# One bf16 place per token instead of two halves of a rank in a routed two-layer kernel

## Chip, core and metric

The kernel runs on one core of a Trainium2 chip. The metric is device time in microseconds, the median of several runs.

## What is computed

Agent attention over 4 sequences of 11456 tokens with 128 channels and 49 agents gives `attn`. Every token whose score against `w_skip` is positive then goes through one of 8 experts, the one with the largest gate logit; the others keep their row.

```python
a2k = sm(agents, k); agent_v = a2k @ v
q2a = sm(q, agents)
attn = q2a @ agent_v
do_compute = attn @ w_skip > 0
xc = attn[do_compute]
e_idx = argmax(xc @ w_gate)
gate_w = softmax(xc @ w_gate)[e_idx]
h = maximum(xc[mask] @ w1[e], 0)
y[mask] = gate_w[mask] * (h @ w2[e])
out[do_compute] = xc + y
```

## The kernel before

A batch is 128 partitions times 90 columns of tokens (`NC` = 90); a token's place in memory is partition x 90 + column. The kernel has two stages.

In the **attention stage** (`attention`) a hand-written order (`ORDER`) walks over chunks of six columns. In one step PE makes the scores of one chunk of keys and one of queries, sums values, and mixes queries (`query_mix`, L446) into the one tile `ps_x`, which DVE divides out and so frees (`query_norm`, L454 and L462). The words `rt` in that order take one step each of the routing generators in `queue`: `codes` finds each token's expert, `count` runs a cumulated sum over the mask of the experts (L540) and gets from it, per partition, the tokens of each expert up to a column (`oin`) and their number (`n`), and `routing` (L566) makes what the expert stage looks up. For this, PE sums `n` over the partitions below and over all (L582). From the sums come the number of 128-token units of each expert (`cnt`), the blocks' starts (`bi`), and for each partition and expert the rank at which it begins (`first`). Adding the starts to the cumulated sums and masking gives every token's rank within its batch (`rk`); POOL does this for the first 72 columns (L604 to L611), DVE for the last 18 (L628, L629). A rank needs two bf16 numbers (`twob`, L635 and L636). The product with `diff` (L646) takes the difference from partition to partition, and DVE stores it in `drow` (L657).

While the last batch is routed, PE works through `items`, a fixed list of products of two blocks of 384 tokens of expert 7 (`layer1`, L739, and `layer2`, L746) that were looked up early (`early`). `static(n)` says how far into that list PE goes before the next routing product stands in its queue: 18 items before the counts (L582), 26 before the `diff` product. A barrier ends the stage, behind ACT's last copy (L751).

The **expert stage** (`experts`) takes blocks of 384 tokens, three units of 128. SP copies for each block the table `drow` of its batch, the starts `first` and the wanted ranks `rank` into `db`, `rf` and `rr` (`fetch`, L988). DVE copies `db` to `dbs` and compares rank and start (`match`, L1085), which gives for each token a column of ones for the partitions that begin at or before it (`hit`). PE multiplies `hit` with the table (`ident_mm`, L1271): the differences add up to the row of ranks of the partition that holds the token, and one column counts up to that partition's number. There are two products per unit, one for each half:

```python
t.matmul(id_ps[:, h, :n], lhsT=m, rhs=dbs[:, h, :n], start=True, stop=False)
w = t.matmul(id_ps[:, h, :n], lhsT=m, rhs=dbs[:, h, n:], start=False, stop=True)
```

DVE compares the row with the wanted rank to find the column (`select_column`, L1096), and makes the token's index from partition and column (`select_token`, L1102 and L1104; `select_id`, L1109). A rank that is not there gets an index out of bounds. POOL gathers the rows by these indices two blocks ahead (L1213) and scatters results (L1227). Around the lookup, PE makes the two layers of the block, three products for each because values are split in two parts (L1296, L1302), ACT takes the upper part `hh` (L1187) and DVE the lower part `hl` (L1122).

DVE's order in a block (`body`, L1150) is: `hl` twice, the selections, `hl`, the token, `hl`, the index, the result of the block before, `hl` four times, the split of x (L1118), `match` for the next block. PE's (`block`, L1307) is: four parts of layer 1, the turned result, the lookup products, then layers 2 and 1 in turn, the transposition of the next x, the rest of layer 2.

Of the kernel before, what the change touches and what calls it, by code (L numbers as in the profile page):

```python
# [8 lines left out]
F32 = mybir.dt.float32  # L9
F32R = mybir.dt.float32r  # L10
BF16 = mybir.dt.bfloat16
# [6 lines left out]
P = 128  # L18
# [12 lines left out]
ROUND = 1.5 * 2.0**23 * P  # L31
# [32 lines left out]
class Shapes:  # L64
# [3 lines left out]
    def __init__(self, b, n):  # L68
# [7 lines left out]
        self.KU = self.NC + NE  # L76
# [15 lines left out]
class Persist:  # L92


    def __init__(self, nc, sh):
# [15 lines left out]
        self.db = over("db", [P, NB, 2 * (sh.NC + 1)], BF16)  # L111
# [10 lines left out]
        self.drow = a("drow", [P, sh.B, 2 * (sh.NC + 1)], BF16).ap()  # L122
        self.first = a("first", [P, sh.B * NE + 1, NB], F32).ap()
# [7 lines left out]
        self.rf, self.rr = (a(x, [P, 2 * NB], F32).ap() for x in ("rf", "rr"))  # L131
# [11 lines left out]
def attention(nc, tc, sh, io, ps):  # L143
# [10 lines left out]
    with ExitStack() as ctx:  # L154
# [55 lines left out]
        while at < sh.NC:  # L210
            n = next((n for n in range(1, sh.NC - at) if sh.COLS[at + n] != sh.COLS[at] + n), sh.NC - at)
            iota(ps.jot[:, at : at + n], [[1, n]], 1 + sh.COLS[at], 0)
# [3 lines left out]
        nc.vector.memset(ps.first, float(INVALID))  # L216
# [4 lines left out]
        nc.vector.memset(ps.drow, 0.0)  # L221
        nc.vector.memset(ps.drow[:, :, sh.NC], 1.0)
        for b in range(1, sh.B):
            x = ps.drow[:, b, 2 * sh.NC + 1 :]
            nc.vector.tensor_scalar(x, ps.ident[:, 0:1], float(P * b), None, op0=ALU.mult)
# [340 lines left out]
        def routing(b):  # L566
# [7 lines left out]
            if not last:  # L574
# [16 lines left out]
            starts = ps.first[:, b * NE : (b + 1) * NE, :]  # L591
            start = starts[:, :, 0]
            v.scalar_tensor_tensor(out=starts, in0=bi[:, :NE].unsqueeze(2).to_broadcast([P, NE, NB]), scalar=float(P),
                                   in1=pt[:, :NE].unsqueeze(2).to_broadcast([P, NE, NB]), op0=ALU.mult, op1=ALU.add)
            yield
            a = [rt.tile([P, NE], F32, name=f"a{i}") for i in range(2)]
            v.tensor_tensor(out=a[0], in0=start, in1=oin0[:, :NE], op=ALU.subtract)
            v.tensor_tensor(out=a[1], in0=start, in1=n0, op=ALU.add)
# [793 lines left out]
```

## Time and profile before

| | us |
|---|---|
| median of 3 runs (lowest, highest) | 720.91 (720.17, 721.12) |
| the profiled execution | 720.13 |
| its span, first to last instruction | 718.4 |
| busy: PE | 683.7 |
| busy: DVE | 500.4 |
| busy: ACT | 369.4 |
| busy: POOL | 361.0 |

The span is what the trace covers; 1.7 us of the execution lie around it. A matmul's end is modelled, so the starts of successive products tell more than their durations. PE's weight loads are listed as an engine of their own (PEld) and overlap the products. An idle time in brackets stands before the instruction of its row, with what ended it. The attention stage ends at 356 us; the expert stage has 37 blocks from 358 us on.

### The profile page before, as it was taken

What the parts mean: (1) busy time and instruction counts of PE and PEld (TensorE: products, weight loads), DVE (VectorE), ACT (ScalarE), POOL (GpSimd) and SP (SyncE); (2) the same over time, 40 slices, a digit from 0 to 9 for tenths busy, and PEclk for the clock granted to TensorE, in tenths of its full rate; (3) what the DMA queues carried; (4) which work ended last, traced back from release to release, by engine and by line L of the source; (5) the groups of instructions that cost most, each with busy time, mean ns of one, the idle gap of its engine ahead of it and who ended that gap; (6) DMA issues with size and microseconds to landing.
All of it is one profiled execution on the core that took longest, in us unless ns stands there. A gap on an engine that the chain in (4) does not pass through costs nothing. (4 is left out here: it accounts for less than half of the span.)

```text
span 718.4 us, 18098 instructions
## 1 busy us (share of the span) xinstructions
PE 683.7 (95%) x5447; PEld 635.5 (88%) x5447; DVE 500.4 (70%) x1694; ACT 369.4 (51%) x1036; POOL 361.0 (50%) x457
## 2 busy tenths in 40 slices
PE   6999999999989899889799999999999999999995
PEld 6988989898878788776489999999999999999995
DVE  4423445666679789887567777787777777777784
ACT  2443555545444555665245555555555555555552
POOL 3455323232424443442176666666666666666663
PEclk9999999999999999999999999999999999999998
DMA  8999989999988968672122222122222222221210
GB/s 314 388 388 396 328 290 363 332 321 299 372 277 288 314 212 274 242 261 104 52 58 63 54 50 56 53 56 56 60 56 60 60 60 56 56 60 51 53 40 18
DMA packets 80350, 123.83 MB, mean 172 GB/s; under 512 B 35798, under 2 KB 43994, under 8 KB 80288
## 3 DMA queue, kind: packets, MB, share of 16 engines
q1 hardware_dynamic: 63872, 84.76, 36.4%
q10 hardware_dynamic: 8928, 23.79, 8.5%
q0 software_dynamic: 7488, 14.54, 6.7%
q8 instruction: 29, 0.48, 0.3%
q14 instruction: 33, 0.27, 0.1%
HBM read 87.18 MB, written 31.50 MB: 165 GB/s over the span
## 5 line engine op out<-in xcount | busy, mean ns | idle before, releaser
L1187 ACT ACTIVATE hh<-h 128x384 fp32r<-128x384 f32 x296 | 145.0, 491 | 97.2 <-ACTq L936 92.8
L1122 DVE SCALAR_TENSOR_TENSOR hl<-h,hh 128x384 fp32r<-128x384 f32 x296 | 155.6, 551 | 45.1 <-DVEq L936 42.1
L1213 POOL DMA_INDIRECT xg<-out_dram,ids x108 | 110.8, 1026 | 83.9 <-issue 73.2
L1227 POOL DMA_INDIRECT out_dram<-xo,sid x117 | 116.4, 995 | 45.3 <-issue 34.5
L1302 PE MATMUL y<-hh,w 128*128 128x384 f32 x512 | 137.1, 349 | 0.0
L425 ACT ACTIVATE qe<-ps_s,qm 128x49 f32<-128x49 f32 x360 | 75.7, 311 | 116.8 <-DVE qm L419 116.8
L1296 PE MATMUL h<-xh,w 128*128 128x384 f32 x512 | 130.8, 337 | 1.1 <-PEq L936 1.1
L333 PE MATMUL ps_s<-agT,ld 128*128 128x128 f32 x960 | 124.5, 284 | 5.7 <-DMA ld<-in_k_dram 5.7
L333 PEld LDWEIGHTS ps_s<-agT,ld 128*128 128x128 f32 x960 | 114.2, 195 | 12.9 <-issue 7.1
L1296 PEld LDWEIGHTS h<-xh,w 128*128 128x128 f32 x512 | 92.5, 188 | 1.6 <-issue 1.6
L1302 PEld LDWEIGHTS y<-hh,w 128*128 128x128 f32 x512 | 89.0, 189 | 0.1
L1296 PE MATMUL h<-xl,w 128*128 128x384 f32 x256 | 86.3, 337 | 0.0
L1302 PE MATMUL y<-hl,w 128*128 128x384 f32 x256 | 86.0, 336 | 0.0
L349 DVE TENSOR_TENSOR run<-scores,run 128x294 f32<-128x294 f32 x56 | 28.7, 512 | 81.3 <-ACT scores L344 77.9
L446 PE MATMUL ps_x<-av,eT 50*128 50x138 f32 x720 | 58.8, 294 | 10.5 <-DVE G L462 9.3
L446 PEld LDWEIGHTS ps_x<-av,eT 50*128 50x128 f32 x720 | 47.0, 186 | 21.9 <-issue 12.4
L462 DVE TENSOR_TENSOR xs<-ps_x,qr 128x768 f32<-128x768 f32 x60 | 57.5, 959 | 9.1 <-DMA out_dram<-xs 5.1
L333 PE MATMUL ps_s<-agT,lds 128*128 128x128 f32 x480 | 60.7, 279 | 0.0
L333 PEld LDWEIGHTS ps_s<-agT,lds 128*128 128x128 f32 x480 | 56.0, 192 | 2.9 <-issue 0.7
L505 POOL COPY xs<-gs 128x6 f32<-128x6 f32 x60 | 10.5, 205 | 75.2 <-issue 49.1
L1296 PEld LDWEIGHTS h<-xl,w 128*128 128x128 f32 x256 | 48.1, 188 | 0.0
L1183 ACT ACTIVATE yT<-y 128x384 f32<-128x384 f32 x37 | 18.2, 492 | 58.1 <-ACTq L936 58.1
(202 smaller groups left out, 1105.7 us busy)
## 6 DMA issues: line engine op xcount, KB each, us to landing
out_dram<-xs ACTq DMA_DIRECT2D x60, 387.0 KB, 5.3
ld<-in_q_dram SPq DMA_DIRECT2D x44, 384.0 KB, 5.0
ld<-in_v_dram SPq DMA_DIRECT2D x38, 387.0 KB, 5.3
ld<-in_k_dram SPq DMA_DIRECT2D x36, 384.0 KB, 6.0
lds<-in_k_dram SPq DMA_DIRECT2D x24, 384.0 KB, 6.6
lds<-in_v_dram SPq DMA_DIRECT2D x22, 387.0 KB, 5.4
ld<-in_moe_w_dram SPq DMA_DIRECT2D x24, 256.0 KB, 5.4
lds<-in_q_dram SPq DMA_DIRECT2D x16, 384.0 KB, 5.2
```

Of the source, the lines that this page charges most:

```text
L333: r.append(ten.matmul(pt[:, t * NA : t * NA + P], lhsT=xT[:, t * P : (t + 1) * P], rhs=agT[:, b, :], start=True, stop=True))
L349: vec.tensor_tensor(out=run, in0=stored(n), in1=run, op=ALU.max)
L425: act.activation(qes[n % PAR["qe"]][:, t, :NA], s[:, t, :], AF.Exp, bias=mx[:, t : t + 1])
L446: ten.matmul(px[:, h, t, :], lhsT=eT[s, t * P : (t + 1) * P], rhs=st["av", b][s, :], start=True, stop=True)
L462: vec.tensor_tensor(out=out[:r, h, j, :], in0=px[:r, h, j, w], op=ALU.mult, in1=rs[:r, h, j].unsqueeze(3).to_broadcast(list(px[:r, h, j, w ...
L1122: v.scalar_tensor_tensor(out=hl[:, f], in0=h_ps[f % HB], scalar=0.0, in1=hh[:, f], op0=ALU.max, op1=ALU.subtract).then_inc(sem["HL"], 1)
L1183: s.activation(yT, y_ps, AF.Copy).then_inc(sem["YS"], 1)
L1187: s.activation(hh[:, f], h_ps[f % HB], AF.Relu).then_inc(sem["HH"], 1)
L1213: g.indirect_dma_start(out=xg[n % TURN][:, h, :], out_offset=None, in_=out, in_offset=bass.IndirectOffsetOnAxis(ap=ids[:, n % TURN, h : h ...
L1227: g.indirect_dma_start(out=out, out_offset=bass.IndirectOffsetOnAxis(ap=sid[:, n % 2, h : h + 1], axis=0), in_=xo[:, n % 2, h, :], in_offs ...
L1296: w = t.matmul(h_ps[f % HB], lhsT=ps.w1[e][wx][:, cs], rhs=x, start=(n == 0), stop=(n == 2))
L1302: w = t.matmul(y_ps, lhsT=ps.w2[e][wx][:, f, :], rhs=h[:, f], start=(f == 0 and n == 0), stop=(f == FC - 1 and n == 2))
```

## The change

A token is no longer looked up by its rank among all tokens of its batch, but by its place among the tokens of its partition, counted over experts. That is at most 90, so one bf16 number holds it. For each batch, expert and partition a record of three numbers (`rec`) takes the place of `first`: how many tokens of this expert the partitions below have, how many all have, and a shift, the step from partition to partition in what must be taken off the wanted rank to get the place. The shift comes out of the same `diff` product, which has 8 columns more for it (98 instead of 180 in all). The blocks' starts, the ranks' starts and the split into halves go; POOL's two sums no longer need the counts of all partitions and move ahead of them; two additions (`rhs`, `every`) and a copy (`rec`) come in, and `routing` takes fewer steps of the order for a batch.

```diff
+            rhs = rt.tile([P, NC + NE], BF16, name="rhs")
+            every = rt.tile([P, NE], F32, name="every")
+            v.tensor_tensor(out=rhs[:, NC:], in0=oin0[:, 1:], in1=oin1[:, 1:], op=ALU.add)
+            v.tensor_tensor(out=every, in0=n0, in1=n1, op=ALU.add)
+            big = part[0][0]
+            ahead = oin1[:, :NE].unsqueeze(2).to_broadcast([P, NE, NA_])
...
+                static(20)
+            else:
+                pool.tensor_tensor(out=big, in0=big, in1=ahead, op=ALU.add)
+                pool.tensor_tensor(out=big, in0=big, in1=mask[0], op=ALU.mult)
                 yield
                 yield
-            if last:
-                static(18)
             pt = ps_e.tile([P, 512], F32, name="ps_e")
...
-            bi = rt.tile([P, NE + 1], F32, name="bi")
-            v.memset(bi[:, 0:1], 0.0)
-            v.tensor_tensor_scan(bi[:, 1:], onesb[:, :NE], cnt, 0.0, ALU.mult, ALU.add)
...
-            v.tensor_tensor(out=a[0], in0=start, in1=oin0[:, :NE], op=ALU.subtract)
-            v.tensor_tensor(out=a[1], in0=start, in1=n0, op=ALU.add)
-            v.tensor_tensor(out=a[1], in0=a[1], in1=oin1[:, :NE], op=ALU.subtract)
...
+            rec = ps.rec[:, b * NE : (b + 1) * NE, :]
+            v.tensor_copy(rec[:, :, :2].rearrange("p e x -> p x e"), pt[:, : 2 * NE].rearrange("p (x e) -> p x e", x=2))
...
-            v.tensor_scalar(twob[:, 0, :], rk, ROUND, -ROUND, op0=ALU.add, op1=ALU.add)
-            v.tensor_tensor(out=twob[:, 1, :], in0=rk, in1=twob[:, 0, :], op=ALU.subtract)
...
-                static(26)
+                static(27)
...
-            ten.matmul(pd[:, : 2 * NC], lhsT=diff, rhs=twob.rearrange("p x j -> p (x j)"), start=True, stop=True)
+            ten.matmul(pd[:, : NC + NE], lhsT=diff, rhs=rhs, start=True, stop=True)
...
-            v.tensor_copy(dr, pd[:, : 2 * NC].rearrange("p (x j) -> p x j", x=2))
+            v.tensor_copy(ps.drow[:, b, :NC], pd[:, :NC])
+            v.scalar_tensor_tensor(out=rec[:, :, 2], in0=pd[:, NC : NC + NE], scalar=-1.0, in1=every, op0=ALU.mult, op1=ALU.add)
...
-                v.tensor_copy(dbs, db).then_inc(sem["RF"], NB)
+                v.tensor_copy(dbs[:, :, : sh.NC + 1], db).then_inc(sem["RF"], NB)
+                at = slice((n - 1) % 2 * NB, (n - 1) % 2 * NB + NB)
+                v.tensor_tensor(out=past, in0=rr[:, at], in1=rf[:, at, 1], op=ALU.is_gt).then_inc(sem["V1"], 1)
+                v.tensor_copy(dbs[:, :, sh.NC + 1], rf[:, at, 2])
                 for h in range(NB):
-                    x = record(n, h)
-                    w = v.tensor_scalar(hit[:, h * P : (h + 1) * P], ps.iota, rr[:, x], rf[:, x], op0=ALU.add, op1=ALU.is_ge)
+                    if h == NB - 1:
+                        take(v, "V1")
+                        v.scalar_tensor_tensor(out=want, in0=past, scalar=float(INVALID), in1=rr[:, at], op0=ALU.mult, op1=ALU.add)
+                    x = at.start + h
+                    w = v.tensor_scalar(hit[:, h * P : (h + 1) * P], ps.iota, rr[:, x : x + 1], rf[:, x, 0:1], op0=ALU.add, op1=ALU.is_ge)
...
+            def select_rank():
                 take(v, "IDP")
+                v.tensor_tensor(out=goal, in0=want, in1=id_ps[:, :, sh.NC + 1], op=ALU.subtract).then_inc(sem["V1"], 1)
...
-                    t.matmul(id_ps[:, h, :n], lhsT=m, rhs=dbs[:, h, :n], start=True, stop=False)
-                    w = t.matmul(id_ps[:, h, :n], lhsT=m, rhs=dbs[:, h, n:], start=False, stop=True)
+                    w = t.matmul(id_ps[:, h, : sh.NC + 2], lhsT=hit[:, h * P : (h + 1) * P], rhs=dbs[:, h, :],
+                                 start=True, stop=True)
```

In `fetch`, SP's copy of the table has 91 numbers a partition and unit instead of 182, that of the record three instead of one. The early lookups (`early`) change in the same way: of their two products a unit, the second has one column instead of 91.

PE's queue at the end of the attention stage, before: `ps_a`, `ps_s` and `ps_x` are written by the list of fixed products (`layer2`, `layer1`), `ps_e` by the routing.

```order
L582 MATMUL ps_e<-n_4356,onesb 128x8
L746 MATMUL ps_a<-ld_93,ld_88 128x384
L739 MATMUL ps_s<-run,ld_92 128x384
L746 MATMUL ps_a<-ld_95,ld_88 128x384
L739 MATMUL ps_s<-run,ld_92 128x384
L746 MATMUL ps_a<-ld_95,ld_88 128x384
L739 MATMUL ps_s<-run,ld_92 128x384
L746 MATMUL ps_x<-ld_89,ld_94 128x384
L646 LDWEIGHTS diff
L643 TENSOR_LOAD cnt
L644 TENSOR_LOAD cnt
L646 MATMUL ps_e<-twob,diff 128x180
```

And with the change:

```order
L593 MATMUL ps_e<-n_4336,onesb 128x8
L732 MATMUL ps_a<-ld_95,ld_88 128x384
L725 MATMUL ps_s<-run,ld_92 128x384
L732 MATMUL ps_a<-ld_95,ld_88 128x384
L725 MATMUL ps_s<-run,ld_92 128x384
L732 MATMUL ps_x<-ld_89,ld_94 128x384 x2
L630 LDWEIGHTS diff
L627 TENSOR_LOAD cnt
L628 TENSOR_LOAD cnt
L630 MATMUL ps_e<-rhs,diff 128x98
```

Between the counts and the `diff` product stand six products of the list instead of seven, and ahead of the counts two more than before (20 items instead of 18).

DVE's queue in one block of the expert stage, before (`junk` is the column selection, `t` the token, `xo` the result of the block before):

```order
L1122 SCALAR_TENSOR_TENSOR hl<-h,hh 128x384 x2
L1096 SCALAR_TENSOR_TENSOR junk,jp<-id,rr,jot 128x90 x3
L1122 SCALAR_TENSOR_TENSOR hl<-h,hh 128x384
L1102 SCALAR_TENSOR_TENSOR t<-id,jp 128x3
L1104 TENSOR_SCALAR t<-jp 128x3
L1122 SCALAR_TENSOR_TENSOR hl<-h,hh 128x384
L1109 SCALAR_TENSOR_TENSOR ids<-t 128x3
...
L1118 TENSOR_TENSOR xl<-x,xh 128x384
L1087 COPY dbs<-db 128x546
L1090 TENSOR_SCALAR hit<-iota,rr,rf 128x128 x3
```

And with the change:

```order
L1109 SCALAR_TENSOR_TENSOR hl<-h,hh 128x384 x2
L1085 TENSOR_TENSOR goal<-want,id 128x3
L1109 SCALAR_TENSOR_TENSOR hl<-h,hh 128x384
L1090 SCALAR_TENSOR_TENSOR junk,jp<-id,goal,jot 128x90 x3
L1109 SCALAR_TENSOR_TENSOR hl<-h,hh 128x384
L1096 SCALAR_TENSOR_TENSOR ids<-id,jp 128x3
...
L1071 COPY dbs<-db 128x3x91
L1073 TENSOR_TENSOR past<-rr,rf 128x3
L1074 CAST dbs<-rf 128x3
L1080 TENSOR_SCALAR hit<-iota,rr,rf 128x128 x2
L1078 SCALAR_TENSOR_TENSOR want<-past,rr 128x3
L1080 TENSOR_SCALAR hit<-iota,rr,rf 128x128
```

`goal` stands where the selections were, the selections where the token's two operations were, and three operations on three numbers stand between the table's copy and the last `hit`.

POOL's queue in the third batch around the two sums of the routing (`cum`), before; `shared` and `late` are the low parts of the weights of experts 6 and 7:

```order
L492 TENSOR_TENSOR G<-G,top 128x12x8
L320 TENSOR_TENSOR late<-ld_90,late 128x512
L505 COPY xs<-gs 128x6 x2
L610 TENSOR_TENSOR cum_3649<-cum_3649,a_3909 128x576
L611 TENSOR_TENSOR cum_3649<-cum_3649,mask_191 128x576
L320 TENSOR_TENSOR late<-ld_92,late 128x512
L492 TENSOR_TENSOR G<-G,top 128x12x8
L320 TENSOR_TENSOR late<-ld_94,late 128x512
```

And with the change:

```order
L318 TENSOR_TENSOR shared<-ld_94,shared 128x512
L503 COPY xs<-gs 128x6 x2
L586 TENSOR_TENSOR cum_3636<-cum_3636,oin_3789 128x576
L587 TENSOR_TENSOR cum_3636<-cum_3636,mask_190 128x576
L318 TENSOR_TENSOR shared<-ld_88,shared 128x512
L490 TENSOR_TENSOR G<-G,top 128x12x8
L318 TENSOR_TENSOR late<-ld_90,late 128x512
```

The two sums stand two steps of the order earlier, beside the counting of the last columns, and no longer follow `a`.

## Rows read from the trace of the kernel before

**Rows 1.** Busy time by stretch: stretch, length, then PE, PEld, DVE, ACT, POOL, PEclk, DMA.

```profile
345.00:360.00 15.00, 11.90 (x45) 7.56 (x45) 7.16 (x34) 3.78 (x8) 3.31 (x6) 0.98 0.01 2
...
500.00:550.00 50.00, 50.00 (x321) 49.60 (x320) 39.42 (x139) 27.14 (x59) 32.92 (x33) 1.00 0.21 56
```

**Rows 2.** Timeline of an expert block, PE: start, duration, line, operation.

```profile
505.14 0.10 PEld L1277 LDWEIGHTS id<-dbs,hit 128*128 128x128 bf16 x1
505.25 0.20 PE L1277 MATMUL id<-dbs,hit 128*128 128x91 bf16 x1
...
505.47 0.21 PE L1278 MATMUL id<-dbs,hit 128*128 128x91 bf16 x1
...
505.50 0.60 PE L1302 MATMUL y<-hh,w 128*128 128x384 f32 x2
...
514.62 0.20 PE L1277 MATMUL id<-dbs,hit 128*128 128x91 bf16 x1
```

**Rows 3.** One line of the kernel: ACT's copy L1183, ns min/median/max, first and last start.

```profile
L1183 ACT ACTIVATE yT<-y x37: 490/492/492, 370.8 to 710.0; 128x384 f32<-128x384 f32 x37
```

**Rows 4.** Timeline of the same block, DVE and POOL.

```profile
502.27 0.29 DVE L1087 COPY dbs<-db 128x546 bf16<-128x546 bf16 x1
...
504.29 1.08 DVE L1122 SCALAR_TENSOR_TENSOR hl<-h,hh 128x384 fp32r<-128x384 f32 x2 [1.06 <-DVEq L936]
...
509.27 1.05 POOL L1213 DMA_INDIRECT xg<-out_dram,ids  x1 [1.70 <-issue]
```

**Rows 5.** One line of the kernel: DVE's index L1109.

```profile
L1109 DVE SCALAR_TENSOR_TENSOR ids<-t x37: 145/161/164, 364.1 to 705.0; 128x3 int32<-128x3 f32 x37
```

**Rows 6.** Timeline between the stages.

```profile
345.16 0.17 PE L582 MATMUL ps_e<-n,lower 128*128 128x8 bf16 x1 [1.31 <-DVE n L547]
...
345.96 0.81 PE L739 MATMUL ps_s<-run,ld 128*128 128x384 f32 x2
...
346.61 0.81 PE L746 MATMUL ps_a<-ld,ld 128*128 128x384 f32 x2
...
349.93 0.21 DVE L635 TENSOR_SCALAR twob<-rk 128x90 bf16<-128x90 f32 x1
...
350.48 0.24 PE L646 MATMUL ps_e<-twob,diff 128*128 128x180 bf16 x1 [0.49 <-DVE twob L636]
...
355.64 0.48 ACT L751 COPY yT<-ps_x 128x384 f32<-128x384 f32 x1 [2.10 <-PE ps_x L746]
...
358.06 0.59 PE L1296 MATMUL h<-xh,late 128*128 128x384 f32 x2 [2.46 <-PEq L936]
...
366.57 0.52 ACT L1174 ACTIVATE xa<-xg 128x384 f32<-128x384 f32 x1 [4.89 <-DMA xg<-out_dram,ids]
```

**Rows 7.** Waits by engine and line: total us, times, longest.

```profile
PE ps_x L446 <- DVE G L462: 9.3, 11, 1.6
...
DVE dbs L1087 <- DVEq L936: 7.1, 1, 7.1
```

**Rows 8.** Timeline of the third batch's routing: PE, DVE and POOL.

```profile
306.13 0.15 DVE L585 TENSOR_SCALAR nb<-ps_e 128x8 int32<-128x8 f32 x1
...
307.19 1.15 POOL L610 TENSOR_TENSOR cum<-cum,a 128x576 f32<-128x576 f32 x1 [0.79 <-DVE a L598]
307.22 1.14 DVE L599 TENSOR_TENSOR a<-a,oin 128x8 f32<-128x8 f32 x1
...
309.78 0.98 PE L446 MATMUL ps_x<-av,eT 50*128 50x138 f32 x12 [1.33 <-DVE G L462]
...
310.08 1.20 DVE L626 TENSOR_REDUCE rk<-cum 128x72 f32<-128x576 f32 x1
...
313.03 0.97 PE L446 MATMUL ps_x<-av,eT 50*128 50x138 f32 x12 [0.41 <-DVE G L462]
...
314.32 0.40 DVE L631 TENSOR_REDUCE rk<-cum 128x18 f32<-128x144 f32 x1
...
316.61 0.97 PE L446 MATMUL ps_x<-av,eT 50*128 50x138 f32 x12 [0.67 <-DVE G L462]
```

More of the change, by code (lines that the diff above doesn't have):

```diff
@@ L220, in attention @@
             nc.vector.memset(x, 0.0)
[L221 to L225, printed above, removed]
+        for b in range(sh.B):
+            nc.vector.tensor_scalar(ps.drow[:, b, sh.NC :], ps.ident[:, 0:1], float(sh.OUT + P * b - 1), 1.0,
+                                    op0=ALU.mult, op1=ALU.add)
         KA = NA + 1
@@ L672, in routing @@
                 v.tensor_scalar(ps.rr[:, :NB], ps.rank[:, :NB], at, None, op0=ALU.add)
-                pool.tensor_copy(ps.rf[:, :NB], ps.first[:, 0, :])
+                pool.tensor_copy(ps.rf[:, :NB, :], ps.rec[:, 0, :].unsqueeze(1).to_broadcast([P, NB, 3]))
+                st["shift"] = one.tile([P, 1], BF16, name="shift")
+                v.tensor_copy(st["shift"], ps.rec[:, 0, 2:])
         def early(x):
@@ L681, in early @@
             for h in range(NB):
-                vec.tensor_scalar(hit[:, h * P : (h + 1) * P], ps.iota, rank[:, h : h + 1], ps.first[:, 0, 0:1],
+                vec.tensor_scalar(hit[:, h * P : (h + 1) * P], ps.iota, rank[:, h : h + 1], ps.rec[:, 0, 0:1],
                                   op0=ALU.add, op1=ALU.is_ge)
+            want = rt.tile([P, NB], F32, name="want")
+            vec.tensor_scalar(want, rank, ps.rec[:, 0, 1:2], float(INVALID), op0=ALU.is_gt, op1=ALU.mult)
+            vec.tensor_tensor(out=want, in0=want, in1=rank, op=ALU.add)
             yield
@@ L687, in early @@
             for h in range(NB):
-                for y in range(2):
-                    ten.matmul(idp[:, h, :n], lhsT=hit[:, h * P : (h + 1) * P], rhs=ps.drow[:, 0, y * n : (y + 1) * n],
-                               start=(y == 0), stop=(y == 1))
+                m = hit[:, h * P : (h + 1) * P]
+                ten.matmul(idp[:, h, :n], lhsT=m, rhs=ps.drow[:, 0, :], start=True, stop=True)
+                ten.matmul(idp[:, h, n : n + 1], lhsT=m, rhs=st["shift"], start=True, stop=True)
             yield
+            vec.tensor_tensor(out=want, in0=want, in1=idp[:, :, n], op=ALU.subtract)
             jp = rt.tile([P, NB], F32, name="jp")
             for h in range(NB):
-                vec.scalar_tensor_tensor(out=pt[:, TB : TB + sh.NC], in0=idp[:, h, : sh.NC], scalar=rank[:, h : h + 1], in1=ps.jot,
+                vec.scalar_tensor_tensor(out=pt[:, TB : TB + sh.NC], in0=idp[:, h, : sh.NC], scalar=want[:, h : h + 1], in1=ps.jot,
                                          op0=ALU.is_equal, op1=ALU.mult, accum_out=jp[:, h : h + 1])
@@ L779, in early_x @@
             behind(vec.tensor_tensor(out=ps.xl, in0=pt, in1=ps.xh, op=ALU.subtract), st["last"])
[L780 removed]
+            behind(pool.tensor_copy(ps.db, ps.drow[:, 0, :].unsqueeze(1).to_broadcast([P, NB, sh.NC + 1])), st["last"])
         n_all = len(chunks)
@@ L915, in experts @@
     rf, rr, db = ps.rf, ps.rr, ps.db
-    dbs = a("dbs", [P, NB, 2 * (sh.NC + 1)], BF16).ap()
+    dbs = a("dbs", [P, NB, sh.NC + 2], BF16).ap()
     hit = a("hit", [P, TB], BF16).ap()
     junk = a("junk", [P, NB, sh.NC], F32).ap()
-    jp, t1, t2 = (a(x, [P, NB], F32).ap() for x in ("jp", "t1", "t2"))
+    jp, past, want, goal = (a(x, [P, NB], F32).ap() for x in ("jp", "past", "want", "goal"))
     ids, xh, xl = ps.ids, ps.xh, ps.xl
@@ L1002, in dummies @@
             def dummies(n):
-                fetch(n, ps.first[:, sh.B * NE, :], ps.rank[:, 0:n], 0)
+                fetch(n, sh.B * NE, ps.rank[:, 0:n], 0)
             def fill(pad):
```

122 lines of the change are left out of this document (46 added, 76 removed).

## The prediction

> **What bounds the kernel now.** I read the busy times by stretch first [rows 1]. PE is the engine to watch: in the expert stage, 500 to 550 us, it is busy 50.00 of 50.00 us, DVE 39.42; at 345 to 360, where the attention stage passes into the expert stage, it drops to 11.90 of 15.00. In the attention stage PE mostly works too, but in 11 places it waits for DVE, 9.3 us in all [rows 7]. So there are three places with different rules, and each edit is costed at its place.
>
> Next comes the timeline of one expert block [rows 2]: the first lookup product of a block starts at 505.25 and that of the next at 514.62, so a block takes 9.37 us, and PE shows no idle time between. The ACT copy at the end of each block [rows 3] stands 37 times, from 370.8 to 710.0: 339.2 us, that is 36 periods with a mean of 9.42.
>
> **Expert blocks: the main term.** The change takes three of the six lookup products out of each block and makes the other three 92 columns wide instead of 91. The first of the six starts at 505.25, the sixth at 505.47: five steps in 0.22 us, 0.044 us each. The one column more is a ninetieth of that, nothing. Three products fewer are 0.132 us a block. PE is never idle there, so this is on the path, with one exception: in the first block ACT is idle 4.89 us for the rows that a gather brings, which PE is to turn [rows 6], and that chain hangs on the start of the stage and not on PE. This leaves 36 blocks: -4.7 us. The bounds: the step from the sixth lookup product to the next product is 0.03 us (505.47 to 505.50), so if only that much goes with each, 36 x 3 x 0.03 = 3.2; with the first block too, 37 x 0.132 = 4.9. I take the steps' own mean.
>
> The Trainium skill ("TensorE: Matmul & The Clock Gate", Back-to-back issue gap) gives some 81 ns for a pair of weight load and product at 128 columns, in a stream of them. By it the term would be 36 x 3 x 81 ns = 8.7 us, an estimate from that page. The trace has 44 ns for the same thing at 91 columns, so the trace is used.
>
> The other engines must follow the shorter block. DVE: the copy of the table (0.29 us [rows 4]) has half the elements; three new operations on three numbers stand in the same stretch, between the split of x and the first `hl` (`past`, the copy of the shift, `want`); a fourth, `goal`, takes the place of two later ones. The nearest row of three numbers has a median of 0.16 us [rows 5], so the stretch grows by 0.48 us at most, before an `hl` ahead of which DVE is idle for 1.06 us [rows 4]: covered, with 0.6 us left. After two `hl` the order becomes goal, `hl`, the three selections, `hl`, indices: the selections move behind the third `hl`, so this one comes earlier and the fourth about as before. The new indices come within 0.2 us of where they came, and POOL, which issues the gathers from them, is idle for 1.70 us ahead of a group [rows 4]. If these covers were gone, each would cost what it exceeds them by, in every block. SP's three transfers a fetch stay three, on the same queue; the first has half the bytes, the second three numbers where one was. They are issued a block ahead: of the 38 copies of the table only the first waited, 7.1 us for the start of the stage [rows 7]; I cost them at nothing. A transfer that came late would show as such a wait in every block.
>
> **Between the stages.** PE goes through a list of fixed products on two blocks while the last batch's routing is done. [Rows 6] show PE idle 1.31 us at 345.16 for the counts `n`, and 0.49 us at 350.48 for `twob`. One product of the list is two instructions of 0.32 us (345.96 to 346.61: 0.65 us). The change puts two more products ahead of the counts (20 items instead of 18): 1.30 us of work moves into a gap of 1.31. After the counts 12 products are left where there were 14. Of these, six stand ahead of the `diff` product where there were seven, so PE comes to it 0.65 us earlier, at about 349.34 instead of 349.99. When is `rhs` ready? `twob` was ready for PE's start at 350.48; six small operations go from the chain (block starts and sums, about 0.15 us each as the row of 8 numbers at 306.13 in [rows 8]: 0.9), so do the two halves (from 349.93 on, 0.5), and one copy of 16 numbers comes in (0.2, as the small rows): 349.3. So the idle time of 0.49 falls to nearly nothing. Together -1.7; since POOL's sums run beside this chain and can hold one DVE operation, I take -1.6 us. Bounds: 0.9 (one operation held by 1.0 us) and 1.8. It reaches the end whole: ACT's copy at 355.64 follows PE's last product, and the expert stage starts 2.4 us after it, at 358.06. The granted clock is 0.98 of the full 2.4 GHz in the slice up to 360 [rows 1], a short fall after PE's idle time; I cost a change of it at nothing, since the first block waits for its gather anyway.
>
> **Attention stage.** PE waits there for DVE's release of its output tile. In the routing of the third batch three such waits follow one another, 1.33, 0.41 and 0.67 us before PE's starts at 309.78, 313.03 and 316.61 [rows 8]. In each step DVE has routing work beside its fixed work. In the first it begins at 306.13 and ends with the addition that starts at 307.22 and takes 1.14, 2.2 us; less the wait of 1.33, some 0.8 us of it cost PE nothing. By the same cover the second step's 1.20 (one reduction) should cost 0.4, and does. After the change the first step has two counts, one copy and two operations on `cum`: three of 0.15 and two of at most 0.40, 1.2 us; the second both reductions, 1.20 + 0.40 = 1.6; the third two small copies, 0.4. So the waits become 0.4 + 0.8 + 0 = 1.2 instead of 2.4.
>
> But the change moves POOL's two sums two steps ahead, next to two new DVE additions (`rhs`, `every`, 0.3 us). In [rows 8] an operation on 8 numbers takes 0.15 us (306.13), but an addition of 8 numbers 1.14: it starts at 307.22, just behind POOL's sum (307.19, 1.15 us), and ends with it. The Trainium skill ("SBUF — State Buffer", SBUF: two separate sides) has a rule for it: DVE with two SBUF inputs and GpSimd share one port pair, and whoever comes second waits for the other's whole instruction. The row agrees, and the rule speaks against this change, since both new additions have two SBUF inputs. If one is held, as one is now, that earlier step costs PE 0.3 + 1.0 - 0.8 = 0.5: 1.7 a batch instead of 2.4, a gain of 0.7. If none is held the gain is 1.2. If both are, by POOL's two sums in turn, the step costs 0.3 + 2.3 - 0.8 = 1.8, and the batch loses 0.6. For three batches that is -2.1, -3.6 or +1.8. In the first two batches PE has keys and values to do in the same steps, so less of DVE's work reaches it; I give the two together half of its gain: 0.7 + 0.3, -1.0 us, in the case that the row shows.
>
> Small edits go together at nothing: of the 24 early lookup products 12 are one column wide instead of 91 (0.04 us each at most), the four `diff` products have 98 columns instead of 180, each of the four early lookups has one small DVE operation more (0.16 us, inside the cover of 0.8 a step), and the memsets of `drow` at the start go, which run while PE waits for its first keys.
>
> **Sum.** -4.7 - 1.6 - 1.0 = -7.3 us. The profiled execution took 720.13, which gives 712.8; the median of the three runs is 0.78 above it, 720.91, which gives 713.6 us.
>
> **Rivals.**
> Lookups hidden. The weight load for the product behind them is the longer chain, and three products fewer only uncover it. Then the experts give 0, and 720.9 - 2.6 = 718.3. For it: the two products behind the lookups take 0.60 us [rows 2], more than the lookups' steps would ask. Against: the first of them starts 0.03 us behind the sixth lookup, so it stands behind it and not behind a load of its own.
>
> Both additions held, in each routing: +1.8 instead of -1.0, 716.4. For it: the 1.14 row. Against: POOL's sum needs a copy that DVE ends just ahead of them, so DVE is likely first with at least one.
>
> A pair costs more than its step. The weight load of a lookup takes 0.10 us [rows 2]. If PE's pace in the block were set by the loads in their full length, three fewer would give 0.3 us a block, 10.8 in all: 720.9 - 10.8 - 2.6 = 707.5. The page on TensorE named above points this way, with its 81 ns. Against: the products, each with a load, start 0.044 us apart, so the loads overlap.
>
> Slower: DVE becomes the bound of the block. The new comparison of two SBUF operands stands beside POOL's descriptor work for gathers (1.0 us each). Cover ahead of `hl` is 1.06 us, and the first `hl` ends some 0.6 us before PE asks for it: 1.7 in all. One held operation, 0.48 + 1.0, is still covered; from two on (2.5) each block grows by 0.8 us, 36 x 0.8 = 29: 720.9 + 29 - 2.6 = 747. Against: the present computation of the indices has two SBUF operands in the same stage, and its longest of 37 is 164 ns [rows 5].
>
> **Chances.** Forecast, with the attention stage between none and one addition held: 0.70. Lookups hidden 0.10, both additions held 0.13, a pair dearer than its step 0.03, slower 0.04. A measurement of this kernel can tell about 0.2%, 1.4 us, from no change. The range is 709.8 to 717.4: its lower end is the forecast with all its best bounds, 4.9 + 1.8 + 3.6 = 10.3, from the profiled 720.1; its upper end is both additions held, with 1.0 less from the other terms. It leaves out the hidden lookups, the dearer pair and the slower rival, 0.17 together. Faster by over 0.2% (below 719.5) is nearly all but the slower rival: 0.91; same, where hidden lookups meet held additions: 0.05; slower 0.04.
>
> **What the new profile would show.** Right: 3 lookup products a block, 0.044 us apart, periods of 9.24 us between the ACT copies, PE still at 50 of 50; PE's wait for `n` at 345 gone or below 0.2; ACT's copy at about 354, less what the attention stage gains; PE's waits for DVE nearer 8 than 9.3 us in all. Wrong: periods that stay at 9.37 (hidden lookups), idle time of PE for `hl` (DVE is the bound), 1.1 us rows for `rhs` and `every` (both held), an idle time ahead of POOL's gathers near 0.3 (POOL's issues are the bound).

## The result and the profile after

The changed kernel takes 711.42 us, the median of 4 runs (710.22 to 712.07); the kernel before took 721.01 us in 4 runs beside it (720.17 to 721.53). The ratio is 0.9862, with a 95% interval of 0.984 to 0.9884: 9.6 us faster. The forecast was 713.6 us, in a range of 709.8 to 717.4. The profiled execution took 711.06 us with a span of 709.3; the span before was 718.4, so 9.1 us are to be found in the two traces.

In the rows PE is TensorE with the matrix products, DVE is VectorE, ACT is ScalarE, POOL is GpSimd and SP is SyncE. First the busy time by stretch, in the columns of [rows 1].

```profile
345.00:360.00 15.00, 12.55 (x52) 9.39 (x51) 7.02 (x40) 4.02 (x9) 3.59 (x8) 0.89 0.03 7
500.00:550.00 50.00, 50.00 (x309) 49.61 (x308) 41.40 (x156) 28.08 (x59) 32.25 (x33) 1.00 0.20 50
```

PE is still busy 50.00 of 50.00 us in the expert stage, with 309 products where there were 321, and DVE rises from 39.42 to 41.40. Next one expert block on PE, which answers to [rows 2]; the three lookup products now stand in one row.

```profile
499.51 0.29 PE L1262 MATMUL id<-dbs,hit 128*128 128x92 bf16 x3
499.62 0.59 PE L1287 MATMUL y<-hh,w 128*128 128x384 f32 x2
...
508.74 0.29 PE L1262 MATMUL id<-dbs,hit 128*128 128x92 bf16 x3
```

From the first lookup to the product behind the last it is 0.11 us (499.51 to 499.62) where it was 0.25 (505.25 to 505.50), and a block takes 9.23 us where it took 9.37. The ACT copy that ends a block answers to [rows 3].

```profile
L1170 ACT ACTIVATE yT<-y x37: 491/494/494, 367.1 to 700.9; 128x384 f32<-128x384 f32 x37
```

From the first to the last copy it is 333.75 us (367.15 to 700.90) instead of 339.20: 5.45 us less. DVE and POOL in the same block answer to [rows 4].

```profile
503.40 1.06 POOL L1200 DMA_INDIRECT xg<-out_dram,ids  x1 [1.63 <-issue]
...
505.76 0.29 DVE L1071 COPY dbs<-db 128x273 bf16<-128x273 bf16 x1
505.96 0.15 DVE L1073 TENSOR_TENSOR past<-rr,rf 128x3 f32<-128x3 f32 x1
506.03 0.17 DVE L1074 CAST dbs<-rf 128x3 bf16<-128x3 f32 x1
...
506.55 0.16 DVE L1078 SCALAR_TENSOR_TENSOR want<-past,rr 128x3 f32<-128x3 f32 x1
...
507.77 1.08 DVE L1109 SCALAR_TENSOR_TENSOR hl<-h,hh 128x384 fp32r<-128x384 f32 x2 [0.68 <-DVEq L922]
```

The three new operations have taken 0.38 us of the idle time ahead of `hl` (1.06 to 0.68), and POOL is idle 1.63 us ahead of its gathers where it was 1.70. Between the stages, against [rows 6]:

```profile
342.91 0.35 PE L593 MATMUL ps_e<-n,lower 128*128 128x8 bf16 x2
342.96 0.16 DVE L574 TENSOR_TENSOR rhs<-oin,oin 128x8 bf16<-128x8 f32 x1
342.99 1.15 POOL L579 TENSOR_TENSOR cum<-mask,oin 128x576 f32<-128x576 bf16 x1 [2.69 <-DVE oin L543]
343.08 1.08 DVE L575 TENSOR_TENSOR every<-n,n 128x8 f32<-128x8 bf16 x1
...
347.19 0.20 PE L630 MATMUL ps_e<-rhs,diff 128*128 128x98 bf16 x1
...
351.70 0.48 ACT L737 COPY yT<-ps_x 128x384 f32<-128x384 f32 x1 [2.10 <-PE ps_x L732]
...
354.12 0.59 PE L1281 MATMUL h<-xh,late 128*128 128x384 f32 x2 [2.45 <-PEq L922]
...
362.94 0.52 ACT L1161 ACTIVATE xa<-xg 128x384 f32<-128x384 f32 x1 [4.54 <-DMA xg<-out_dram,ids]
```

Neither the counts (L593) nor the `diff` product (L630) has an idle time ahead of it any more. ACT's last copy comes at 351.70 instead of 355.64. The waits, against [rows 7]:

```profile
PE ps_x L444 <- DVE G L460: 7.5, 9, 1.2
```

And the third batch's routing, against [rows 8]:

```profile
298.62 1.15 POOL L586 TENSOR_TENSOR cum<-cum,oin 128x576 f32<-128x576 f32 x1 [0.17 <-DVE oin L543]
298.66 1.14 DVE L574 TENSOR_TENSOR rhs<-oin,oin 128x8 bf16<-128x8 f32 x1
...
299.72 0.15 DVE L575 TENSOR_TENSOR every<-n,n 128x8 f32<-128x8 bf16 x1
...
301.29 0.98 PE L444 MATMUL ps_x<-av,eT 50*128 50x138 f32 x12 [1.23 <-DVE G L460]
...
304.52 0.72 DVE L598 TENSOR_SCALAR cnt<-nb 128x8 int32<-128x8 int32 x1
...
307.30 0.97 PE L444 MATMUL ps_x<-av,eT 50*128 50x138 f32 x12 [0.40 <-DVE G L460]
...
309.92 0.96 DVE L460 TENSOR_TENSOR xs<-ps_x,qr 128x768 f32<-128x768 f32 x1 [0.72 <-DMA out_dram<-xs]
...
311.15 0.97 PE L444 MATMUL ps_x<-av,eT 50*128 50x138 f32 x12 [0.96 <-DVE G L460]
```

POOL's sum starts 0.04 us ahead of `rhs`, and `rhs` ends with it: one addition held, `every` not, and a new wait of 1.23 us at 301.29. A later count, `cnt`, takes 0.72 us where the first batch has 0.17. Ahead of the wait of 0.96 us, DVE itself stood 0.72 us for the transfer that empties the buffer of `xs`. The 9.1 us by stretch, from the same instructions in both traces:

| Stretch | before, us | after, us | gained |
|---|---|---|---|
| start to the last group of query mixes | 333.31 | 331.25 | 2.06 |
| from there to ACT's last copy of the stage | 22.33 | 20.45 | 1.88 |
| from there to the first expert product | 2.42 | 2.42 | 0.00 |
| from there to the first block's ACT copy | 12.72 | 13.03 | -0.31 |
| the 36 periods | 339.20 | 333.75 | 5.45 |
| the end of the span | 8.42 | 8.42 | 0.00 |

### The profile page after: what moved, and what is told of

Its sections match the earlier page's. It is cut to its first block, busy times and chain, and to the rows that moved or that the text cites. A ratio compares the mean times of both kernels' runs of the same rounds, so it can differ in the third digit from the quotient of the medians.

```text
span 709.3 us, 17989 instructions
## 1 busy us (share of the span) xinstructions
PE 678.1 (96%) x5336; PEld 630.7 (89%) x5336; DVE 510.5 (72%) x1759; ACT 370.0 (52%) x1036; POOL 360.5 (51%) x457
## 5 line engine op out<-in xcount | busy, mean ns | idle before, releaser
L1109 DVE SCALAR_TENSOR_TENSOR hl<-h,hh 128x384 fp32r<-128x384 f32 x296 | 156.1, 554 | 32.3 <-DVEq L922 25.5
```

Of the source, the lines that this page charges most:

```text
L1109: v.scalar_tensor_tensor(out=hl[:, f], in0=h_ps[f % HB], scalar=0.0, in1=hh[:, f], op0=ALU.max, op1=ALU.subtract).then_inc(sem["HL"], 1)
```

## The experiments

The theory after the result: PE's lookup steps give the main part, the list between the stages and the shorter chain behind it 1.9 us, and in the attention stage a gain is cut by the held addition. The rivals are those of the prediction (lookups hidden; a pair that costs its load), and for the attention stage that PE's wait there has another cause.

**The first six runs came from chips that are not like the first.** On two chips the kernel before takes 845 us, not 721. Their attention stages agree with the first chip's to tenths of a microsecond and can be read; their expert blocks take 12 to 13 us and can't be compared with 9.2.

**Six products again** (`e1_six`).

```diff
+                    for _ in range(2):
-                    w = t.matmul(id_ps[:, h, : sh.NC + 2], ...
+                        w = t.matmul(id_ps[:, h, : sh.NC + 2], ...
```

> The changed kernel with each lookup product of the expert stage issued twice, so that a block has six again, of 92 columns; the second writes the same numbers over the first. Compared with the changed kernel (711.4 us). Theory: a product is on PE's path with its step of 0.044 us. Three more in each of 36 blocks cost 36 x 3 x 0.044 = 4.8 us, so about 716.2 us, with block periods of 9.36 us where the changed kernel has 9.23. Rival 1, the lookups are hidden behind the weight loads that follow: nothing, 711.4 us, periods of 9.23. Rival 2, a pair costs its load of 0.10 us: 10.8 us, 722 us, periods of 9.53.

Measured: 848.19 us, ratio to the kernel before 1.0054 (0.9997 to 1.0112). That decides nothing, since the blocks are 12 to 13 us long. It was run again:

> The kernel with the lookup products doubled a second time, since the first runs fell on a chip where the blocks of the expert stage took 12 to 13 us instead of 9.2 to 9.4, in the kernel before and in all changed ones, so that three products more or less could not show. On a chip where the kernel before takes about 721 us: theory (0.044 us a product on PE's path) 4.8 us more than the changed kernel, about 716.2 us, periods of 9.36 us. Rival 1, lookups hidden: 711.4 us, periods of 9.23. Rival 2, a load of 0.10 us a pair: 722 us, periods of 9.53. On a chip where the kernel before takes about 845 us: no difference that can be measured from it.

Another chip, the same picture: 845.69 us beside 845.10, ratio 1.0015 (0.9982 to 1.0047).

**Two half products** (`e2_halves`).

```diff
-                    w = t.matmul(id_ps[:, h, : sh.NC + 2], ..., rhs=dbs[:, h, :], ...
+                    for x in (slice(0, n), slice(n, 2 * n)):
+                        w = t.matmul(id_ps[:, h, x], ..., rhs=dbs[:, h, x], ...
```

> The changed kernel with each lookup product cut into two of 46 columns: as many columns as the changed kernel has, and as many products and weight loads as the one before. It asks what the 0.044 us of a step are paid for. If for each pair of load and product: six steps of 0.044, +4.8 us against the changed kernel's 711.4, periods of 9.36 us. If for columns: six steps of 0.022, no difference, 711.4 us, periods of 9.23. Between the two, if a short product runs into the time of the load beside it.

Measured: 854.78 us, ratio 1.0111 (1.0061 to 1.0161); the total says nothing on PE's path, but the starts can be read. Products of 46 columns start 0.026 us apart (185 steps), those of 92 columns 0.043. Half the columns take 60% of a step. That need not be the price of 46 columns, though: in the trace of before, products of 8 columns follow each other at 0.025 us as well (three between 345.16 and 345.23, and the next product behind them).

```profile
345.16 0.17 PE L582 MATMUL ps_e<-n,lower 128*128 128x8 bf16 x1 [1.31 <-DVE n L547]
345.18 0.19 PE L582 MATMUL ps_e<-n,onesb 128*128 128x8 bf16 x2
345.23 0.57 PE L746 MATMUL ps_a<-ld,ld 128*128 128x384 f32 x1
```

So from 8 to 46 columns the step hardly grows, and only from there to 92 by 0.017 us, which points to a least step of some 0.025 us.

> Each lookup product cut into two of 46 columns, a second time for the same reason. In the first run of it the products started 0.026 us apart, where those of 92 columns start 0.043 apart. By the theory that PE's path is charged by these steps a block becomes longer by 6 x 0.026 - 3 x 0.043 = 0.027 us, 36 blocks by 1.0 us: about 712.4 us and periods of 9.25 us on a chip where the kernel before takes 721. Rival, a fixed price for each pair of load and product: 716.2 us, periods of 9.36.

Measured: 845.83 us beside 845.10, ratio 1.0008 (0.9985 to 1.0031), so the 1.1% of the first run does not come back. The steps are 0.026 us again; what they do to a block of 9.2 us stays unmeasured.

**The additions a step later** (`e3_moved`).

```diff
-            v.tensor_tensor(out=rhs[:, NC:], in0=oin0[:, 1:], in1=oin1[:, 1:], op=ALU.add)
-            v.tensor_tensor(out=every, in0=n0, in1=n1, op=ALU.add)
...
                 yield
+                v.tensor_tensor(out=rhs[:, NC:], in0=oin0[:, 1:], in1=oin1[:, 1:], op=ALU.add)
+                v.tensor_tensor(out=every, in0=n0, in1=n1, op=ALU.add)
                 yield
```

> The changed kernel with the two additions of the routing (rhs and every) moved one step of the hand-written order later in the first three batches, past POOL's two sums; the last batch as it is. Theory: in the changed kernel the first addition starts just behind POOL's sum and is held for its whole length (1.13 us instead of 0.16), which makes PE wait 1.05 us at 177.9 and 1.23 us at 301.3 us. Moved, both additions take 0.16 us, these two waits fall below 0.3 us, and the time falls by 0.7 to 1.1 us a batch: 708.1 to 709.3 us. Rival: PE waits there since the step also has the cumulated sum on DVE, and not for the held addition; then the waits stay above 0.7 us, and the time at 711 to 712 us. Rival on the other side: in the later step an operation of the mixing or POOL's next sum meets the additions, a new wait of 1 us a batch appears, and the time is 711.4 or more.

Measured: 845.49 us, ratio 1.0003 (0.996 to 1.0046), so the trace has to tell. Timeline of the third batch, PE, DVE and ACT:

```profile
299.40 0.97 PE L444 MATMUL ps_x<-av,eT 50*128 50x138 f32 x12
...
299.70 0.68 DVE L575 TENSOR_TENSOR rhs<-oin,oin 128x8 bf16<-128x8 f32 x1
...
301.71 0.96 DVE L460 TENSOR_TENSOR xs<-ps_x,qr 128x768 f32<-128x768 f32 x1 [1.10 <-POOL shared L318]
301.94 0.28 ACT L491 ACTIVATE ex<-G 128x96 f32<-128x96 f32 x1 [1.02 <-POOL G L490]
...
302.64 0.55 PE L431 MATMUL ps_e<-ident,qe 128*128 128x128 f32 x3 [0.73 <-ACT eT L433]
...
306.54 0.98 PE L444 MATMUL ps_x<-av,eT 50*128 50x138 f32 x12 [0.58 <-DVE G L460]
```

The wait of 1.23 us is gone (299.40 has none), so the first rival falls: the held addition made that wait. The second came true in part. `rhs` is still held for 0.68 us, now by the end of POOL's second sum, and PE waits 0.73 us for ACT's `eT` and 0.58 instead of 0.40 for DVE: two mixes later nothing of the microsecond is left. In between ACT stands 1.02 us for POOL's `G`, which comes behind a sum of weights (`shared`) in POOL's queue, and `eT` comes behind that; DVE stands 1.10 us ahead of `xs`, whose buffer a transfer empties. So both are bound by work that the move doesn't make earlier. In the first batch 1.16 us of gain shrink to 0.33 in the same way (both against the same mixes in the trace of `e10_still`, counted from the first mix). The last mix starts at 329.95 us from the span's start; in ten traces with the changed kernel's attention stage it lies at 330.86 to 333.08, mean 331.7. From the first mix to the last it takes 249.40 us, as much as the shortest of those ten (249.41, `e10_still`). So the move gains between nothing and 1.7 us, where 2.1 to 3.3 were expected. The hold is what PE waits for at that place, but it isn't what limits the next steps; for the third batch the trace points to ACT's and DVE's waits, which no run took away.

**Copies in the old place** (`e9_copies`): the move of the last run, and beside POOL's sums two copies instead.

```diff
+                v.tensor_copy(rhs[:, NC:], oin1[:, 1:])
+                v.tensor_copy(every, n1)
```

> The kernel with the two additions moved a step later, and in their old place, beside POOL's sums, two copies of the same sizes with one operand in SBUF each; the true additions overwrite what they write. It asks what in the old place was held. Theory (two operands from SBUF make DVE wait for POOL's whole instruction): the copies take 0.15 to 0.2 us, and PE's waits at 178 and 301 us stay below 0.4 us, as they were with the additions moved. Rival (any DVE operation on SBUF that starts behind POOL's sum is held): the first copy takes 1.1 us, and PE's waits of 1.05 and 1.2 us are back. Read from the attention stage, which runs alike on all chips so far.

Measured: 837.51 us in a single run, so the trace alone counts. In the third batch:

```profile
298.58 1.15 POOL L593 TENSOR_TENSOR cum<-cum,oin 128x576 f32<-128x576 f32 x1 [0.17 <-DVE oin L543]
298.61 1.14 DVE L581 CAST rhs<-oin 128x8 bf16<-128x8 f32 x1
...
301.24 0.97 PE L444 MATMUL ps_x<-av,eT 50*128 50x138 f32 x12 [1.22 <-DVE G L460]
```

The copy is held as the addition was, in all three batches (1.137 to 1.140 us), and PE's waits are back, 1.05 and 1.22 us. My theory as written falls: two operands are not needed. The rival, that every operation is held, isn't right as stated either: in the trace of `e3_moved` a reduction of `G` from SBUF (the on-chip memory) on DVE takes 0.24 us at 176.16, in the midst of POOL's second sum. The Trainium skill ("SBUF — State Buffer", SBUF: two separate sides) has the fuller rule, of which the prediction used half: DVE contends with GpSimd when it has two SBUF inputs, or when it runs in a mode that uses both its ports. The copy's rows agree with that second half, with 1.14 us; which mode the copy ran in no trace shows. The changed kernel has such a row too: `cnt<-nb`, with one operand, takes 0.68 to 0.77 us in three of its four batches, beside an operation of POOL, and 0.17 in the first.

**The list's old numbers** (`e4_static`): 18 and 26 for 20 and 27.

> The changed kernel with the numbers 18 and 26 of the kernel before in place of 20 and 27, so that two products of the fixed list go back behind the counts and one behind the diff product. Theory: the list filled PE's wait for the counts; PE again waits some 1.3 us for n, nothing else absorbs it, and ACT's last copy of the stage comes 1.3 us later than in the changed kernel (counted from the end of the attention steps): 712.7 us. Rival: the routing chain's shortening alone pays between the stages, and these numbers pay nothing: 711.4 us, with the wait for n moved to another place.

Measured: 846.16 us, ratio 1.0 (0.9957 to 1.0044). The timeline between the stages:

```profile
342.91 0.17 PE L593 MATMUL ps_e<-n,lower 128*128 128x8 bf16 x1 [1.30 <-DVE n L545]
...
352.74 0.48 ACT L737 COPY yT<-ps_x 128x384 f32<-128x384 f32 x1 [2.10 <-PE ps_x L732]
```

The wait for `n` is back with 1.30 us, and from the last mix to ACT's copy it takes 21.67 us instead of 20.45: 1.22 us of the 1.88 belong to the two numbers together, the other 0.66 to the shorter chain. The rival, that they pay nothing, falls.

**What holds the expert blocks on the other chips.** In the trace of `e3_moved`, PE, POOL and DVE in one block:

```profile
558.33 1.02 POOL L1219 DMA_INDIRECT out_dram<-xo,sid  x1 [0.30 <-issue]
...
559.41 0.29 PE L1267 MATMUL id<-dbs,hit 128*128 128x92 bf16 x3
559.65 1.00 POOL L1219 DMA_INDIRECT out_dram<-xo,sid  x1 [0.30 <-issue]
560.96 0.97 POOL L1219 DMA_INDIRECT out_dram<-xo,sid  x1 [0.30 <-issue]
563.28 0.16 DVE L1090 TENSOR_TENSOR goal<-want,id 128x3 f32<-128x3 f32 x1 [2.54 <-DVEq L927]
```

The lookups end at 559.70, and DVE, idle for 2.54 us, starts `goal` at 563.28. On the first chip `goal` follows the lookups by 0.15 us (508.74 + 0.29 to 509.18). In between, in the trace of `e3_moved`, POOL issues the three scatters of a block. So the scatters were taken out (`e7_quiet`), and six products were tried without them (`e8_quiet_six`).

```diff
-                    g.indirect_dma_start(out=out, ..., in_=xo[:, n % 2, h, :], ...).then_inc(sem[f"SC{n % 2}"], 16)
+                g.inc_swdge_sem([sem[f"SC{n % 2}"]], [16 * NB], mode="add")
```

> The changed kernel without POOL's scatters in the expert stage: the results of the experts are computed and not written. On the chips of the first runs (kernel before: 845 us) the blocks take 12 to 13 us, and while POOL issues the scatters, ACT learns of PE's finished products up to 4 us late. Theory: without the scatters that delay goes, PE sets the block again, and the periods are 9.2 us there too; the time falls to 705 to 712 us. Rival: the delay has another cause (the gathers, the code of the engines, the chip), periods stay above 11 us, and the time above 780 us.

> As the run without scatters, and with each lookup product issued twice, six a block. Difference of the two runs. Theory: three products more on PE's path with a step of 0.044 us, 36 x 3 x 0.044 = 4.8 us more, and periods 0.13 us longer. Rival 1, lookups hidden: no difference. Rival 2, a load of 0.10 us a pair: 10.8 us more, periods 0.30 longer. If the blocks without scatters are still above 11 us long, this pair tells nothing.

Measured: 716.13 us where the kernel before takes 836.57 (ratio 0.856, 0.8524 to 0.8596), and 716.99 us with six products. The long blocks are gone, and so is the delay:

```profile
504.31 0.29 PE L1260 MATMUL id<-dbs,hit 128*128 128x92 bf16 x3
...
504.78 0.15 DVE L1085 TENSOR_TENSOR goal<-want,id 128x3 f32<-128x3 f32 x1
```

But the time is above the 705 to 712 us expected, and the periods go to and fro between 8.9 and 10.4 us, so this pair doesn't price the products: the 36 periods take 342.91 us with three and 344.48 with six. Left were the gathers. They went too, in the same way, in three kernels: the changed one (`e10_still`), the changed one with six products (`e11_still_six`), the one before (`e12_still_before`).

> The changed kernel without the gathers and the scatters of the expert stage: POOL only passes the semaphores on, and the experts work on rows of zeros. Without scatters alone the delay of PE's signals was gone, but the periods still went to and fro between 8.9 and 10.4 us. Theory: with POOL's transfers gone altogether PE sets every block, as on the chip of the first result: regular periods of 9.2 us. The first block also no longer waits 4.5 us for gathered rows, so the time is 705 to 711 us. Rival: something else of these chips stretches the block; periods stay irregular.

> As the run without gathers and scatters, with each lookup product issued twice, six a block: the difference of the two is the price of three products a block. Theory: a step of 0.044 us each on PE's path, periods 0.13 us longer, 36 or 37 x 0.132 = 4.8 to 4.9 us more. Rival 1, the lookups are hidden: no difference. Rival 2, a load of 0.10 us a pair: periods 0.30 us longer, 10.8 to 11.1 us more.

> The kernel before, without the gathers and scatters of the expert stage: its difference to the changed kernel without them is the change's whole effect where PE sets the block. Theory: three products a block, 4.8 us, and 1.9 us between the stages and 1.2 us in the attention stage as the traces of the first result had them: 7.9 us more, with periods as long as in the run with six products. Rival: the other edits on DVE and SP have a part in the block's period, which the run with six products then does not reach; the periods differ by over 0.03 us.

Measured on one chip: 704.00 us (702.91 to 707.83, 6 runs), 708.97 us (708.01 to 710.37) and 712.50 us (712.19 to 713.87). The ACT copy at the end of a block, in that order:

```profile
L1170 ACT ACTIVATE yT<-y x37: 491/494/494, 364.8 to 698.5; 128x384 f32<-128x384 f32 x37
```

```profile
L1170 ACT ACTIVATE yT<-y x37: 491/494/494, 365.7 to 704.1; 128x384 f32<-128x384 f32 x37
```

```profile
L1183 ACT ACTIVATE yT<-y x37: 490/492/492, 368.0 to 707.1; 128x384 f32<-128x384 f32 x37
```

The blocks are regular again. The 36 periods take 333.70, 338.42 and 339.16 us, with a median of 9.23, 9.36 and 9.37. So three products a block are worth 4.72 us, 0.131 a block. Lookups hidden would give 0, loads of 0.10 us would give 10.8; both rivals fall. Between six products and the kernel before there are 0.74 us more, 0.02 a block, under the 0.03 that I set for a part of the other edits. A block of `e11_still_six` shows where a part of it lies:

```profile
509.07 0.41 PE L1258 MATMUL id<-dbs,hit 128*128 128x92 bf16 x6
509.31 0.60 PE L1283 MATMUL y<-hh,w 128*128 128x384 f32 x2
```

Its six products take 0.24 us to the product behind them, those of the kernel before 0.25; by the median of all blocks 0.234 and 0.246. So two products on the same `hit` that write the same numbers are 0.012 us a block cheaper than the two halves were, about 0.4 of the 0.74; the rest lies in the first five periods and the last.

The change's whole effect without the transfers is 8.5 us by the medians, near the 7.9 expected, but not by its terms: by the traces the blocks give 5.5 where 4.8 were expected, the way up to the last mix 2.1 where 1.2 were, and the first block takes 0.7 back.

The time of `e10_still`, 704.00, lies a microsecond below what was expected. Its trace keeps PE's clock at 1.00 of full speed through the start of the expert stage, where after PE's idle time the first result's trace has 0.69 from 355 to 360 us, and `e11_still_six` 0.50 (1.2 GHz) from 356 to 358. From the first expert product to the first block's ACT copy `e11_still_six` takes 11.27 us and `e10_still` 10.39, clock and products together. `e12_still_before`, whose clock stays at 1.00 as well, takes 9.71. The changed kernel's first block is thus 0.7 us longer once no gather holds it. DVE's first `hl` there starts 2.72 us behind the first expert product (1.97 in `e12_still_before`), as the copy of the table starts later (0.77 us behind that product, against 0.23) and the new operations stand ahead of `hl`. PE stands idle meanwhile:

```profile
357.84 0.59 PE L1282 MATMUL y<-hh,late 128*128 128x384 f32 x2 [0.64 <-PEq L922]
```

## Why the prediction was right, point by point

**Experts, -4.7.** Measured -5.45 on the first chip, -5.46 without transfers. The step's price was right: three products are worth 4.72, against 36 x 0.132 = 4.75. The remaining 0.74 I had not seen, and it brings the term above its bound of 4.9. About 0.4 of it are the halves' dearer steps (0.246 us for the six, against 0.234); the cause of that, and of the rest, stays open.

**The pair's price.** The Trainium skill's 81 ns for a pair ("TensorE: Matmul & The Clock Gate", Back-to-back issue gap) would have made 8.7 us, by estimate. The runs have 44 ns (4.72 us / 108 products), as the trace of before had. The same page of the Trainium skill (Wait — 56ns, not 53.3ns?) has a second rule for products that follow each other: columns by 2.4 GHz and some 2.5 ns, an estimate of 41 ns for 92 columns and 22 ns for 46. The 43 ns measured at 92 columns agree with that one. The 26 ns at 46 columns tell less, since 8 columns take 25. In this short run of lookups, then, a product isn't charged its load of 0.10 us.

**Covers in the block.** Right: the new operations took 0.38 us of the 0.48 allowed, `past` was held in none of 38 (151 to 157 ns), and POOL kept 1.63 us ahead of its gathers. One term did not come: the copy of the table has half the elements and still takes 0.29 us. It cost nothing, since it lies in the same cover. Nor was it only the first copy of the table that waited: four did, 9.4 us in all, the later three 0.5 to 1.0 us each, at no cost in the periods. In the first block the cover doesn't hold, as `e10_still` shows; on the first chip that block's gather hides it.

**First block.** Taken as bound by its gather, so no gain; it became 0.31 us longer (12.72 to 13.03). The gathered rows came 3.1 us after the last gather's start, before 2.8.

**Between the stages, -1.6.** Measured -1.88, just beyond the bound of 1.8. Both waits went (1.31 and 0.49, together 1.80). The held operation for which I took off a tenth or two was there, `every` with 1.08 us, but PE had products of the list to do while it lasted.

**Attention stage, -1.0.** The case "one held" came in all three batches (`rhs` 1.13 us, `every` 0.15). In the third batch the waits forecast as 0.5, 0.4 and 0.8 were 1.23, 0.40 and 0.96. The step that failed is the cover of 0.8 us that was taken off in each of them. It was read from a single step (2.23 us less the wait of 1.33, which makes 0.9 and not 0.8), and its test on a second one, "should cost 0.4, and does", was luck: there DVE stood 0.42 us for the transfer that empties `xs`. So it did in the third wait after the change; `e10_still`, with the same attention stage, has 0.44 us there, as the transfer holds DVE for only 0.19.

```profile
311.80 0.96 DVE L462 TENSOR_TENSOR xs<-ps_x,qr 128x768 f32<-128x768 f32 x1 [0.42 <-DMA out_dram<-xs]
```

```profile
310.08 0.96 DVE L460 TENSOR_TENSOR xs<-ps_x,qr 128x768 f32<-128x768 f32 x1 [0.19 <-DMA out_dram<-xs]
...
311.31 0.98 PE L444 MATMUL ps_x<-av,eT 50*128 50x138 f32 x12 [0.44 <-DVE G L460]
```

In the first of the three steps there was no cover left: it also holds the cumulated sum (0.97 us, at 297.37), which the prediction left out, and the 1.14 of `rhs` with the 0.15 of `every` came back nearly whole as PE's wait of 1.23. PE's waits for DVE fell to 7.5 us in 9 places; I had said nearer 8 than 9.3. From the first mix to the last, the profiled pair gains 1.15 us (251.14 to 249.99). The first mix starts anywhere from 80.55 to 82.17 us in fourteen traces, whatever the kernel, so the other 0.91 us of the profiled 2.06 can be chance: over all traces the last mix starts at 333.4 us before (2 traces) and 331.7 after (10), 1.7 us earlier.

**The sum.** -7.3 forecast, -9.1 in the traces: 0.75 more from the experts, 0.3 more between the stages, 1.06 more up to the last mix, 0.3 less in the first block. Each of the three terms came out larger than it was put, and the range held. For the blocks and between the stages that is the mechanism as forecast, with sizes off by 0.75 and 0.3; in the attention stage the time came out near for other reasons than the ones given, so its size is luck in part.

**What the prediction had no place for** is the chip. On the chips where scatters stretch the blocks, the nearest kin of the changed kernel, `e4_static` and `e3_moved`, are at 1.0 and 1.0003 of the kernel before: a gain that can't be measured. The changed kernel itself was not timed there. On those chips PE, named as the engine to watch at the start of the prediction, isn't the bound of the expert stage.

## What to carry to other kernels

Where the trace shows an engine without idle time in a loop, the spacing of the instruction starts is the price of taking some out; it held here to 0.02 us in a block. A wait that was filled from a list of independent work paid nearly in full (1.22 us for a wait of 1.30), but a wait removed in a chain of several engines was found again two steps on, where others stood in the way. A cover (work that costs nothing because others are busy longer) that is read from one step needs a second step to confirm it, and a look at what else held the engine there. Look at which chip the numbers come from: what bounds a stage can change with it, and with it the worth of the change.

## What the runs showed of the hardware that I had not expected

- On four chips with the kernel before at 835 to 845 us, products of PE in the expert stage are followed up late while POOL issues scatters: `goal` starts 3.6 us after the lookups' modelled end. The changed kernel takes 716 us without scatters and 704 without gathers too. Whether PE's signals or PE's products are late can't be told, since the ends of products are modelled; why the first chip doesn't show it is open.
- A DVE copy of 8 numbers a partition, one operand, from f32 to bf16, that starts just behind an addition of POOL lasts as long as that: 1.14 us, as long as an addition of two operands.
- A copy of 273 bf16 numbers in three rows takes 0.29 us, one of 546 in one piece 0.29 to 0.30.
